# Channel attention over a 113 MB image on one core: the first six rows of the last store go as three transfers of fewer partitions

## The chip, the cores and the metric

The kernel runs on one core of a Trainium2 chip. The metric is the device time of one execution in microseconds (us), the median of several runs. Three runs of the kernel before gave 720.6, 720.0 and 720.54 us, a median of 720.54 us. The profile is of one more execution, which took 720.05 us; its span, from the first recorded instruction to the last, is 718.3 us.

## What is computed

```python
x, w1d   # x: bf16 (1, 384, 384, 384), last axis = channels; w1d: bf16, one number
g = einsum("bhwc->bc", x) / (H * W)        # mean of each channel
s = sigmoid(g * w1d[0])                    # k = 1: no neighbours
out = x * s[:, None, None, :]
```

Every element of the output needs the mean of its channel, so all of x has to be read before the first output element can be made. x has 113 MB and the kernel's on-chip tile holds 275 of its 1152 rows (the unit of the next section), so most of x is read twice.

## The kernel before, in words

The image is seen as 1152 rows of 384 channels for each of 128 partitions (147,456 pixels over 128). All data lives in one on-chip tile, `arena`, of 128 partitions by `ROWS` rows by 384 channels; a row is 768 bytes of one partition.

The rows of x are divided into four runs (`RUNS`, L226): run 0 has the first `N_FIRST` = 43 rows, the next has the rest of what is streamed, and the last two hold what stays on chip. Inside a run of n rows each partition owns n neighbouring rows of DRAM (`view`, L213), so a transfer of m rows of a run moves one piece of m x 768 bytes for each partition it covers.

The work has two halves. In the first, loads bring all rows of x in; TensorE sums them over the partitions (`sum_rows`), and some rows are kept, partly folded so that four rows take the place of three (`fold`). Then ScalarE makes s. In the second half every row is multiplied by s on VectorE (`scale`, L482, its instruction on L487) and stored (`store`, L493, its DMA on L499): first the rows that were kept, unfolded where needed (`unfold`), and then the streamed rows, loaded once more (`load`, L248, its DMA on L255) and stored. Streamed rows are taken from the end of x towards its beginning, so run 0 is the last to be loaded, scaled and stored.

All loads and stores are issued by SyncE (SP), in program order. `Flow` (from L21) records each step with what it reads and writes and puts in the waits; each SP transfer takes one of 24 semaphores in turn (`LANES`), and a transfer also waits for the one 24 before it on the queue. At the end SP waits for the last transfer of each of the 24. A transfer's semaphore counts to 16.

The order of loads, scalings and stores in the second half comes from a planner at build time, the `while True` loop at the end. It keeps its own clock `now`, puts transfers with an estimated cost into `moves`, and a finished scaling into `waiting` by `send(at, a, n, then)`: `at` is the first row of x, `a` the place in the arena, `n` the number of rows. When such an entry is due, the loop calls `store(at, a, n)` (L751). A load is cut into parts of at most `PART` = 16 rows for scaling; run 0 with its 43 rows is scaled as 14, 14 and 15 rows and sent as one store with `at` = 0. It is the only store with `at` = 0, and it is the last transfer of the program.

Of the kernel before, what the change touches and what calls it, by code (L numbers as in the profile page):

```python
# [129 lines left out]
def kernel(  # L130
# [11 lines left out]
    nc = tc.nc  # L142
    P = nc.NUM_PARTITIONS
# [50 lines left out]
    arena = pool.tile([P, ROWS, C], bf16, name="arena")  # L194
# [13 lines left out]
    of = out.rearrange("b h w c -> (b h w) c")  # L208
# [4 lines left out]
    def view(t, r0, n):  # L213
        return t[r0 * P : (r0 + n) * P, :].rearrange("(p r) c -> p r c", r=n)

    def rows(lo, n):
        return [("a", r) for r in range(lo, lo + n)]
# [11 lines left out]
    def run_of(i):  # L229

        return next(run for run in reversed(RUNS) if i >= run[0])
# [171 lines left out]
    def copy_bank(src, dst, reads, writes):  # L403
        fl.add(
            "ACT", lambda: nc.scalar.copy(dst.bitcast(u32), src.bitcast(u32)), reads=reads, writes=writes  # L405
        )

    for i, bk in enumerate(banks):
        lo, hi = i * BANK, min((i + 1) * BANK, PS * C)
# [72 lines left out]
    def scale(a, n, eng="DVE", s=s_bf, after=()):  # L482
        v = arena[:, a : a + n, :]
        vec = nc.vector if eng == "DVE" else nc.gpsimd
        fl.add(
            eng,
            lambda: vec.tensor_tensor(  # L487
                out=v, in0=v, in1=s[:, None, :].to_broadcast([P, n, C]), op=Op.mult
            ),
            reads=rows(a, n) + ["s_bf" if s is s_bf else "bank0"], writes=rows(a, n), after=after,  # L490
        )

    def store(at, a, n):  # L493
        r0, m = run = run_of(at)
        lo, hi = at - r0, at - r0 + n
        assert hi <= m
        return fl.add(
            "SP",
            lambda: nc.sync.dma_start(out=view(of, *run)[:, lo:hi, :], in_=arena[:, a : a + hi - lo, :]),  # L499
            reads=rows(a, hi - lo), dma=True,  # L500
        )

    def unfold(k, first):

        g, lo, p = pieces[k]
        a, at = first + 3 * lo, first + 3 * GROUPS[g][1] + lo
        w, wc = flat(a, 3 * p), [rows(a + j * p, p) for j in range(3)]
        w0, w1, w2 = (flat(a + j * p, p) for j in range(3))
        ba, ca = Y, Y + PIECE
        u, b, c = flat(at, p), flat(ba, p), flat(ca, p)  # L510
        uc, bc, cc = rows(at, p), rows(ba, p), rows(ca, p)

        def fields():
            bits(u, w2, SHR, 3, AND, 0x0F00, wc[2], uc)
            bits(b, w0, SHR, 7, OR, 0x780F, wc[0], bc)
            bits(c, w1, SHR, 11, OR, 0x78F0, wc[1], cc)
            join(b, b, c, AND, bc + cc, bc)
            join(u, u, b, Op.add, uc + bc, uc)

        def three():  # L520
            wall = wc[0] + wc[1] + wc[2]
            bits(w, w, AND, 0x87FF, OR, 0x3800, wall, wall)
            scale(a, 3 * p)

        def fourth():

            bits(u, u, AND, 0x87FF, XOR, 0x3F77, uc, uc)
            scale(at, p + (at + p == first + N_BANKED - 1 and g == BANKED))

        return [  # L530
            (fields, 3 * TS(p) + 2 * TT(p)),
            (three, TS(3 * p) + TT(3 * p)),
            (fourth, TS(p) + TT(p)),
        ]
# [4 lines left out]
    def TT(n):  # L539
        return 0.15 + 0.2 * n  # L540
# [55 lines left out]
    BIG, CAP, PART, LOW, LAST = 32, 48, 16, 9.0, 4.0  # L596
    BANKS_AT = 2
    N_SPLIT = 2
    now = dve_at = 0.0
    moves, waiting, over, acts = deque(), deque(), deque(), deque()  # L600
    landed = deque()
# [7 lines left out]
    def runs():  # L609
        near = {i for g in list(line)[:N_NEAR] if g in TOPS for i in range(TOPS[g], TOPS[g] + GROUPS[g][1])}  # L610
        got, i = [], 0
        while i < ROWS:
            if idle[i] and i not in near:
                j = i
                while j < ROWS and idle[j] and j not in near:
                    j += 1
                got.append((j - i, i))
                i = j
            else:
                i += 1  # L620
        return got

    def send(at, a, n, then, known=None):

        waiting.append((dve_at, n, then, at, a, [] if known is None else known))

    def backlog():
        return sum(e[1] for e in moves) + ROW * sum(e[1] for e in waiting)
# [10 lines left out]
    def stored(a, n):  # L639

        def f():
            for i in range(a, a + n):
                unused.discard(i)
                if not Y <= i < Y + 8:
                    idle[i] = True
        return f
# [30 lines left out]
    def start_group():  # L677
# [35 lines left out]
        sent = 0  # L713
        if len(line) >= total - N_SPLIT and q == PAIR:

# [7 lines left out]
    while True:  # L723

        if dve_at <= now:
            ahead = backlog()
            can = bool(turns)
            if not can and not alongside and (ahead >= PENDING or not landed):
                can = start_group()
            if landed and (ahead < PENDING or not can):  # L730
                a, at, n, end = landed.popleft()
                scale(a, n, s=s_ps if alongside and now else s_bf)
                dve_at = now + TT(n)
                since = (a, at) if since is None else since
                if end or ahead < MERGE:
                    b, first = since
                    send(first, b, at + n - first, stored(b, at + n - first))
                    since = None
            elif can:
                f, t, then = turns.popleft()  # L740
                f()
                dve_at = now + t
                if then:
                    then()
        if alongside and alongside[0][0] <= now:
            _, a, at, n = alongside.popleft()
            store(at, a, n)
            moves.append([now + LAT, n * ROW + PER_STORE, stored(a, n)])
        while waiting and waiting[0][0] <= now:
            _, n, then, at, a, known = waiting.popleft()  # L750
            known.append(store(at, a, n))  # L751
            moves.append([now + LAT, n * ROW + PER_STORE, then])
        if not asked and not line and not turns:
            verdict()
            asked = True
        if out_rows == total and not checked:
            checked = True
            fl.add("POOL", again, reads=["odd_i", "s_bf"], writes=rows(Y, N_OVER), after=written, bare=True)
        while over and over[0][0] <= now:
            over.popleft()[1]()  # L760

        got = runs()
        if bank_at is None and len(line) <= total - BANKS_AT and got and max(got)[0] >= N_BANKED:
            a = max(got)[1]
            for i in range(a, a + N_BANKED):
                idle[i] = False
            back = arena[:, a : a + PS, :].rearrange("p r c -> p (r c)")
            for i, bk in enumerate(banks):
                lo, hi = i * BANK, min((i + 1) * BANK, PS * C)
                copy_bank(bk[:, 0 : hi - lo], back[:, lo:hi], [("bank", i)], rows(a, PS))  # L770
            for lo, hi, at, cell in PARTS:
                copy_bank(at, arena[:, a + N_BANKED - 1, lo:hi], [], rows(a + N_BANKED - 1, 1) + [cell])
            bank_at = (a, now + 5.0)
            got = runs()

        if got and todo < N_STREAM:
            n, a = max(got)
            left = N_STREAM - todo
            left -= run_of(left - 1)[0]
            n = min(n, CAP, left)  # L780
            ahead = backlog()
            if (todo or not (landed or alongside or waiting)) and (n >= BIG or n == left or (ahead < LOW and n >= 8) or ahead < LAST):

                lo = N_STREAM - todo - n
                load(lo, a, n)
                for i in range(a, a + n):
                    idle[i] = False
                parts = [(a + e, lo + e, f - e, f == n) for e, f in split(n, PART)]
                todo += n
                moves.append([now + LAT, n * ROW + PER_LOAD, lambda parts=parts: landed.extend(parts)])  # L790

        if moves and moves[0][0] <= now:
            moves[0][1] -= DT
            if moves[0][1] <= 0:
                over.append((now + SEEN, moves.popleft()[2]))
        else:
            stall += DT
        if not (alongside or moves or waiting or over or landed or line or turns) and todo == N_STREAM:
            break
        now += DT  # L800
# [34 lines left out]
```

## Time and profile before

| | |
|---|---|
| median of three runs | 720.54 us (720.0 to 720.6) |
| the profiled execution | 720.05 us |
| its span | 718.3 us |
| HBM read, written | 189.92 MB, 113.25 MB |
| mean DMA rate over the span | 422 GB/s |
| busy share: PE, DVE, ACT, POOL | 30%, 68%, 17%, 1% |
| the last store's issue, and its size | 691.8 us, 4128 KB |

How to read it: times are counted from the start of the span. Engines are PE (TensorE), DVE (VectorE), ACT (ScalarE), POOL (GpSimd), SP (SyncE). DMA work is done by 16 DMA engines that all queues share; a DMA share of 1.00 (or 100%) over a stretch means that all 16 were moving packets all the time. A packet is counted whole in the stretch in which it starts, so that the share of a short stretch can be somewhat above or below the true one. "DMA to landing" is the time from SP's issue to the last count of the transfer's semaphore; where earlier transfers still wait on the DMA engines, it includes that waiting.

### The profile page before, as it was taken

How to read it: one execution, taken by the hardware profiler on the slowest of the kernel's cores; microseconds unless marked ns; L12 is line 12 of the kernel's file. 1: busy time of each engine (PE TensorE's matmuls, PEld its weight loads, DVE VectorE, ACT ScalarE, POOL GpSimd, SP SyncE). 2: the span in 40 equal slices, each digit the busy share in tenths (PEclk: the TensorE clock that was granted, in tenths of full speed). 3: DMA queues.
4: the chain of work that ended last, by engine and by line, in shares of the span. 5: the costliest groups of instructions: out<-in, count | busy, mean ns of one | idle time of the engine just before them, and what ended most of it. 6: DMA issues, size and time to landing. Idle time of an engine off the chain costs nothing.

```text
span 718.3 us, 2042 instructions
## 1 busy us (share of the span) xinstructions
PE 213.0 (30%) x1186; PEld 0.3 (0%) x3; DVE 485.6 (68%) x454; ACT 122.1 (17%) x101; POOL 10.2 (1%) x7
## 2 busy tenths in 40 slices
PE   4776977997868770000000000000000000000000
PEld 0000000000000000000000000000000000000000
DVE  4606270639896819998997999996991999005640
ACT  3604160426674610000002000000000000000000
POOL 0000000000000005000000000000000000000000
PEclk9989889999999995555555555555555555555555
DMA  9999999999999989999999999999999999999997
GB/s 372 443 422 444 434 431 418 447 428 424 428 426 428 425 343 359 413 424 430 425 434 429 433 443 424 435 426 437 434 431 432 443 431 426 436 429 431 447 421 307
DMA packets 21181, 303.30 MB, mean 422 GB/s; under 512 B 2354, under 2 KB 2738, under 8 KB 9010
## 3 DMA queue, kind: packets, MB, share of 16 engines
q1 hardware_dynamic: 21168, 303.18, 98.9%
q8 instruction: 4, 0.07, 0.0%
q14 instruction: 7, 0.06, 0.0%
q10 hardware_dynamic: 2, 0.00, 0.0%
HBM read 189.92 MB, written 113.25 MB: 422 GB/s over the span
## 4 chain that ended last, share of the span: by engine, by line
DMA 54%; DVE 27%; PE 7%; ACT 3%; another core or an unknown queue 2%; POOL 1%; SPq 1%; issue 1%; DVEq 0%; ACTq 0%
DMA arena<-in_x_dram 38%; DVE arena L487 19%; DMA out_dram<-arena 16%; PE bank L261 7%; DVE arena L295 6%; DVE arena L301 3%; ACT arena L332 2%; POOL arena L487 1%; SPq L255 1%; ACT arena L405 1%; SPq L499 0%; ACT s_bf L475 0%; ACT bank L479 0%; ACT bank L405 0%
## 5 line engine op out<-in xcount | busy, mean ns | idle before, releaser
L487 DVE TENSOR_TENSOR arena<-arena,s_bf 128x1536 bf16<-128x1536 bf16 (+9 forms) x100 | 231.0, 2345 | 84.4 <-DMA arena<-in_x_dram 68.2
L261 PE MATMUL bank<-arena,ones 128*128 128x384 bf16 x1151 | 207.1, 341 | 46.7 <-DMA arena<-in_x_dram 46.2
L295 DVE TENSOR_SCALAR arena<-arena 128x1536 uint16<-128x1536 uint16 (+3 forms) x240 | 142.9, 644 | 111.4 <-DMA arena<-in_x_dram 94.9
L332 ACT ACTIVATE arena<-arena 128x3072 uint16<-128x3072 uint16 (+1 forms) x40 | 108.0, 2700 | 111.0 <-DVE arena L295 111.0
L301 DVE TENSOR_TENSOR arena<-arena 128x1536 uint16<-128x1536 uint16 (+2 forms) x100 | 109.3, 1093 | 7.9 <-PE bank L261 4.0
L557 PE MATMUL bank<-odd,ones 128*128 128x1 bf16 x1 | 0.2, 185 | 313.8 <-DVE odd L552 313.8
L405 ACT COPY arena<-bank 128x512 uint32<-128x512 uint32 (+3 forms) x9 | 4.4, 497 | 107.9 <-DMA out_dram<-arena 107.6
L487 POOL TENSOR_TENSOR arena<-arena,s_bf 128x1536 bf16<-128x1536 bf16 (+1 forms) x3 | 10.0, 3351 | 269.4 <-ACT bank L479 269.4
L487 DVE TENSOR_TENSOR arena<-arena,bank 128x1536 bf16<-128x1536 bf16 (+3 forms) x8 | 9.4, 1250 | 0.0
L405 ACT COPY bank<-arena 128x512 uint32<-128x512 uint32 (+3 forms) x9 | 4.1, 494 | 26.3 <-PE bank L261 26.2
L332 ACT ACTIVATION_READ_ACCUMULATOR arena<-arena 128x1 f32 x40 | 7.5, 186 | 0.0
L261 PE MATMUL bank<-zeros,ones 128*128 128x384 bf16 x32 | 5.5, 326 | 0.0
L475 ACT ACTIVATE s_bf<-bank,w_sc 128x384 bf16<-128x384 f32 x1 | 0.6, 580 | 13.9 <-PE bank L261 13.9
L275 PE MATMUL bank<-arena,ones 128*128 128x384 bf16 x1 | 0.5, 477 | 7.2 <-DMA arena<-in_x_dram 7.2
L803 ACT ACT_TABLE_LOAD x1 | 1.3, 1283 | 0.7 <-PEq L819 0.7
L362 DVE TENSOR_SCALAR w_sc<-bank 128x1 f32<-128x1 f32 x1 | 0.2, 159 | 1.1 <-PE bank L357 1.1
L352 DVE MEMSET ones<- 128x128 bf16 x1 | 0.2, 165 | 1.0 <-SPq L107 1.0
L357 PE MATMUL bank<-w_bf,ones 1*128 1x1 bf16 x1 | 0.2, 178 | 2.2 <-DMA w_bf<-in_w1d_dram 2.2
L557 PEld LDWEIGHTS bank<-odd,ones 128*128 128x128 bf16 x1 | 0.1, 103 | 572.9 <-DVE odd L552 572.9
L561 DVE CAST odd_i<-bank 128x1 int32<-128x1 f32 x1 | 0.2, 157 | 0.3 <-PE bank L557 0.3
L479 ACT COPY bank<-s_bf 128x192 uint32<-128x192 uint32 x1 | 0.3, 323 | 0.0
L547 DVE TENSOR_REDUCE worst<-seen 128x1 f32<-128x40 f32 x1 | 0.2, 188 | 0.0
(8 smaller groups left out, 0.9 us busy)
## 6 DMA issues: line engine op xcount, KB each, us to landing
arena<-in_x_dram SPq DMA_DIRECT2D x16, 4608.0 KB, 29.9
out_dram<-arena SPq DMA_DIRECT2D x9, 3072.0 KB, 24.1
out_dram<-arena SPq DMA_DIRECT2D x5, 4608.0 KB, 35.8
arena<-in_x_dram SPq DMA_DIRECT2D x7, 2304.0 KB, 19.8
arena<-in_x_dram SPq DMA_DIRECT2D x14, 1152.0 KB, 17.0
arena<-in_x_dram SPq DMA_DIRECT2D x5, 3072.0 KB, 15.2
arena<-in_x_dram SPq DMA_DIRECT2D x18, 768.0 KB, 8.9
arena<-in_x_dram SPq DMA_DIRECT2D x2, 4512.0 KB, 29.4
```

The lines of the kernel that those rows point to most:

```text
L255: lambda: nc.sync.dma_start(out=arena[:, a : a + hi - lo, :], in_=view(xf, *run)[:, lo:hi, :]),
L261: return pe.add_instruction(mybir.InstMatmult(name=nc.get_next_instruction_name(), ins=[pe.lower_ap(rhs), pe.lower_ap(ones[:])], outs=[pe. ...
L275: return nc.tensor.matmul(acc, lhsT=ones[:], rhs=arena[:, i, :], start=first, stop=last)
L295: lambda: nc.vector.tensor_scalar(out=dst, in0=src, scalar1=s0, scalar2=s1, op0=op0, op1=op1),
L301: "DVE", lambda: nc.vector.tensor_tensor(out=dst, in0=a, in1=b, op=op), reads=reads, writes=writes
L332: lambda: nc.scalar.activation(out=y, in_=y, func=ACTF.Copy, accum_out=seen[:, 2 * k + i : 2 * k + i + 1]),
L405: "ACT", lambda: nc.scalar.copy(dst.bitcast(u32), src.bitcast(u32)), reads=reads, writes=writes
L475: lambda: nc.scalar.activation(out=s_bf[:], in_=acc, func=ACTF.Sigmoid, scale=w_sc[:, 0:1]),
L479: "ACT", lambda: nc.scalar.copy(s_ps.bitcast(u32), s_bf[:].bitcast(u32)), reads=["s_bf"], writes=["bank0"]
L487: lambda: vec.tensor_tensor(out=v, in0=v, in1=s[:, None, :].to_broadcast([P, n, C]), op=Op.mult),
L557: lambda: nc.tensor.matmul(votes, lhsT=ones[:], rhs=odd[:], start=True, stop=True),
L803: nc.scalar.preload_act_table(ACTF.Sigmoid)
```

## The change

The store with `at` = 0 is written as four stores of the same bytes: three of the first six rows, for the partitions 0 to 12, 13 to 63 and 64 to 127 (13, 51 and 64 partitions), and one of the other 37 rows for all 128 partitions. All other stores are as before.

```diff
-    def store(at, a, n):
+    def store(at, a, n, p0=0, p1=P):
         r0, m = run = run_of(at)
         lo, hi = at - r0, at - r0 + n
         assert hi <= m
         return fl.add(
             "SP",
-            lambda: nc.sync.dma_start(out=view(of, *run)[:, lo:hi, :], in_=arena[:, a : a + hi - lo, :]),
+            lambda: nc.sync.dma_start(
+                out=view(of, *run)[p0:p1, lo:hi, :], in_=arena[p0:p1, a : a + hi - lo, :]
+            ),
             reads=rows(a, hi - lo), dma=True,
         )
+
+    def store_last(at, a, n):
+
+        for p0, p1 in zip(LAST_CUTS, LAST_CUTS[1:]):
+            store(at, a, N_LAST, p0, p1)
+        return store(at + N_LAST, a + N_LAST, n - N_LAST)
...
+    N_LAST, LAST_CUTS = 6, (0, 13, 64, P)
...
-            known.append(store(at, a, n))
+            known.append((store if at else store_last)(at, a, n))
             moves.append([now + LAT, n * ROW + PER_STORE, then])
```

The planner's entry in `moves` stays one entry of 43 rows.

## The prediction, made before the result was known

> **What bounds the kernel now.** I read the page's 40 slices first, then what SP issues at the end, then the packets of the last microseconds. The slices:
>
> ```profile
> span 718.3 us, 2042 instructions
> DMA  9999999999999989999999999999999999999997
> GB/s 372 443 422 444 434 431 418 447 428 424 428 426 428 425 343 359 413 424 430 425 434 429 433 443 424 435 426 437 434 431 432 443 431 426 436 429 431 447 421 307
> ```
>
> The DMA engines are full throughout; only the last slice, 18 us, falls to 307 GB/s. So what the change can win or lose lies in the tail. SP's last stores (start, duration; then issue to landing) and VectorE's last scalings:
>
> ```profile
> 680.15 0.33 SPq L499 DMA_DIRECT2D out_dram<-arena  x1
> 682.85 8.90 DVE L487 TENSOR_TENSOR arena<-arena,s_bf 128x5376 bf16<-128x5376 bf16 x3 [2.73 <-DMA arena<-in_x_dram]
> ...
> 691.78 0.33 SPq L499 DMA_DIRECT2D out_dram<-arena  x1
> ...
> DMA to landing us min/median/max: 24.9/25.9/26.8
> ```
>
> The store ahead of the last is issued at 680.15 and lands 26.8 us later, at 707.0; the last is issued at 691.78 and lands 24.9 us later, at 716.7. For some 15 us the last store only waits behind others, so VectorE and SP are not what ends the kernel: the DMA engines are. Now the tail's packets, in two stretches, 712.7 to 713.36 and 713.36 to 716.36:
>
> ```profile
> DMA packets 14, 0.00 MB, mean 0 GB/s; under 512 B 14, under 2 KB 14, under 8 KB 14
> ...
> DMA packets 6, 0.13 MB, mean 44 GB/s; under 512 B 2, under 2 KB 2, under 8 KB 2
> q1 hardware_dynamic: 6, 0.13, 10.2%
> ```
>
> Every transfer of the SP queue has 128 data packets, one for each partition, and 16 closing packets of a few bytes: the page counts 21168 packets for 87 loads and 60 stores, 144 each.
>
> ```profile
> q1 hardware_dynamic: 21168, 303.18, 98.9%
> q10 hardware_dynamic: 2, 0.00, 0.0%
> ...
> L255 SPq DMA_DIRECT2D arena<-in_x_dram x87: 327/340/1241, 1.0 to 627.3; - x87
> ...
> L499 SPq DMA_DIRECT2D out_dram<-arena x60: 332/332/1252, 270.0 to 691.8; - x60
> ```
>
> So a transfer has one closing packet for each DMA engine it uses, 8 partitions to an engine; w_bf's, of one partition (q10), has one data and one closing packet: one engine. In the tail, then, **fourteen engines close the last store between 712.7 and 713.36, and two close it only about 716.3**, after two data packets each that start after 713.36 (0.13 MB in 4). The kernel ends 3 us later than fourteen of its sixteen DMA engines do. From the last closing at 716.3 it is 0.4 us to the landing, 1.6 more to the end of the span, and 1.75 from there to the 720.05 us of this execution, which stands 0.5 us under the median of 720.54. I add my difference to the median.
>
> **The change part by part.** What an engine takes for one packet comes from stretches with packets of one size (share x 16 x length / packets). Stretches 708 to 712, 695 to 697.5, and 282.9 to 284.3:
>
> ```profile
> q1 hardware_dynamic: 56, 1.85, 106.9%
> ...
> q1 hardware_dynamic: 44, 1.22, 112.8%
> ...
> q1 hardware_dynamic: 146, 0.56, 103.1%
> ```
>
> 33 KB: 1.069 x 64 / 56 = 1.22 us. 27.7 KB: 1.128 x 40 / 44 = 1.025 us. Both are 27 GB/s, so the 37 rows that remain, 28,416 bytes, take 1.05. In the third stretch 130 data packets of 4.3 KB take 0.176 each (16 closings at about 0.01 taken off): 0.18 for the six rows' 4,608 bytes. The two late engines run alone after 713.36 and still need 1.22 (10.2% of 48 engine-us over 4).
>
> *The last store before:* 8 x 1.22 + 0.01 = 9.78 us on each engine.
>
> *After:* each engine has 8 x 1.05 = 8.41 us of the 37 rows, plus small packets. How many depends on how 13, 51 and 64 partitions are divided. The rows show 128 in 16 shares of 8 and 1 as one share, and I take equal shares over as many engines as go into the count: 13 engines of one, 3 of seventeen (51 = 3 x 17), 16 of four. If the engines are always taken from the first on, three have 1 + 17 + 4 = **22 small packets**, ten have 5 and three have 4. [...]
>
> *What a small packet costs* is the open term. Lower end 0.18, from the row above, where each engine serves its own eight partitions. Upper end 0.36, half the rate, if the 27 GB/s belongs not to the engine but to the way into its partitions and two engines must share it. The 64 partitions are what eight engines serve in a full transfer, and sixteen would read them; the 51 belong mostly to engines other than the three, which read them at the same time. No row shows an engine on another's partitions. Two rows are near. A load (639.5 to 644.5) and a store (650.5 to 655.5), both of 36,864-byte packets:
>
> ```profile
> q1 hardware_dynamic: 63, 2.32, 107.4%
> ...
> q1 hardware_dynamic: 64, 2.36, 109.1%
> ```
>
> Both give 1.364 us (1.074 x 80 / 63 and 1.091 x 80 / 64). A limit that is the same for reading HBM and writing it, with sixteen engines at work or two, sits at the engine or at its way into the arena. And small packets at half rate do occur, at 284.4 to 285.9, from a cause that the trace doesn't show: 0.957 x 24 / 79 = 0.29 us for 4 KB.
>
> ```profile
> DMA packets 86, 0.32 MB, mean 213 GB/s; under 512 B 7, under 2 KB 7, under 8 KB 86
> q1 hardware_dynamic: 86, 0.32, 95.7%
> ```
>
> The trace doesn't choose. I take **0.36** as somewhat likelier, since all its full rates are of engines that each have eight partitions to themselves, which the change ends. [...]
>
> *Sum with 0.36.* An engine with 22: 8.41 + 7.92 + 0.04 of closings = 16.37, against 9.78: +6.6. It starts with the fourteen, so it closes not at 712.7 to 713.36 but at 719.3 to 719.95. The late engines with 5: 8.41 + 1.80 + 0.03 = 10.24: +0.46, at 716.8. The last closing moves from 716.34 to 719.3 to 719.95, +3.0 to +3.6; I take +3.4.
>
> *Sum with 0.18.* With 22: 8.41 + 3.96 + 0.04 = 12.41, +2.6, closing at 715.3 to 716.0. Late with 5: 9.34, -0.44; with 4: -0.63. Last closing at 715.9 or so: -0.4.
>
> *The rest.* Three more issues on SP, 0.33 us each, at most 1.25 (the row of L499): 3.8 us at worst, under the 15 us in which the last store waits anyway, so nothing; without that cover up to 3.8. They read rows of the first scaling only (14 rows, 682.85 on, a third of 8.90 us) and can go about 686, ahead of the 37 rows at 691.78; nothing on SP stands between. Their added waits are for transfers 24 back, long landed, and nothing waits for these stores but the end. Closings: one or two more for an engine, 0.01 each, counted above.
>
> **The rivals.**
>
> *A. Small packets keep 0.18 and the late pair is lightened: -0.4.* For it: 27 GB/s is also what an engine alone does, and the three heavy engines fill just the 3 us in which they idle now. Against it: the sharing above. 720.54 - 0.4 = 720.1.
>
> *B. Small packets keep 0.18, but one of the late pair is among the three heavy ones: slower.* No view tells which engines are late. Its place is a late engine with 22 packets; its price is 22 x 0.18 + 8.45 - 9.78 = +2.6 from 716.07 or 716.34: +2.3 to +2.6, 722.8 to 723.1. It decides as soon as a late engine has more than (8 x 0.17) / 0.18 = 7.5 small packets. By count a pair out of 16 misses three given ones in 13 x 12 / (16 x 15) = 65%, so 35%. [...]
>
> *C. B's mishap with 0.36 as well:* 716.34 + 6.6, so +6.6: 727.1.
>
> *D. The division is not in equal shares:* 51 goes as four to an engine on thirteen. Then most engines have 9 small packets, and with 0.18 a late one takes 8.41 + 1.62 + 0.03: +0.3, 720.8 at most.
>
> *E. The lag belongs to the profiled execution alone.* Then the heavy engines would end 2.6 us or more behind the others where none does now. But without the lag the timed runs would be 3 us shorter than 720.05, and they are 720.0 to 720.6.
>
> **How the numbers follow.** I give the shared way 0.55 and the engine's own rate 0.45. By the count of 35%, the first parts into the forecast, 0.36, and C, 0.19. Of the second, 0.05 goes to D and 0.03 to a gain that I don't see (a late engine still has at least 8.41 + 0.72, so -0.63 is the most this balance can give), and the other 0.37 parts into A, 0.25, and B, 0.12. The likeliest is +3.4: **723.9 us**, with its own range 722.6 to 726.0 (a price somewhat under 0.36, or engines slowed in turn on their own partitions). The range reaches down to A with the most it can give, 719.8, and up to 726.0; it leaves out C and the unseen gain. A measurement of this kernel can tell about 0.2%, 1.4 us, from no change: slower by more than that are the forecast, B and C, 0.67; within it A and D, 0.30; faster 0.03.
>
> **What the profile of the changed kernel would show.** The SP queue has 150 transfers, and beyond the full ones' packets 128 small data packets and 13 + 3 + 16 closings if the shares are equal, 13 + 13 + 16 or so in D. In the tail the last closings are three instead of two in the forecast, at about 719.5, with the late pair between them and the others; in A all sixteen close between about 712.4 and 716. The share while small packets run, some 14 us ahead of the end, shows their price directly: 0.18 or 0.36. It would be wrong if the waiting behind earlier stores did not cover the issues (a gap in the DMA share before the last store), or if the late engines were other than two in the timed runs.

## The result and the profile after

The kernel with the change takes 721.78 us, the median of 22 runs (720.87 to 722.99); the kernel before took 720.48 us in 22 runs beside it (719.81 to 722.54). The ratio is 1.0020 with a 95% interval of 1.0015 to 1.0026: 1.3 us slower, and the interval lies above 1; the time is inside the stated range of 719.8 to 726.0, and 38% of the forecast +3.4. The profiled execution took 721.28 us, 1.23 more than that of before.

The page after, its span, slices and SP's queue:

```profile
span 719.5 us, 2045 instructions
...
DMA  9999999999999989999999999999999999999996
GB/s 367 440 425 442 432 432 427 438 430 426 425 428 427 424 340 362 413 424 428 428 432 429 434 433 435 432 431 441 422 443 423 430 437 434 441 430 424 436 428 290
DMA packets 21341, 303.30 MB, mean 422 GB/s; under 512 B 2386, under 2 KB 2770, under 8 KB 9170
...
q1 hardware_dynamic: 21328, 303.18, 98.8%
```

And the count of packets before:

```profile
DMA packets 21181, 303.30 MB, mean 422 GB/s; under 512 B 2354, under 2 KB 2738, under 8 KB 9010
```

The last slice differs most (290 in place of 307 GB/s); no other differs by more than 13. SP's queue has 160 packets more: 128 small ones, and 32 closing packets (2386 against 2354). 32 is 13 + 3 + 16: the transfers of 13, 51 and 64 partitions went over 13, 3 and 16 engines, in the equal shares that the prediction took. With the three always among the thirteen, three engines had 22 small packets; the packets followed by engine, below, agree.

SP's last four issues, and the times from issue to landing of these four stores:

```profile
686.12 1.58 SPq L499 DMA_DIRECT2D out_dram<-arena  x3
...
692.05 0.37 SPq L499 DMA_DIRECT2D out_dram<-arena  x1
...
DMA to landing us min/median/max: 22.5/24.2/25.9
```

The three cut transfers are issued 6 us ahead of the 37 rows, as forecast; their 1.58 us on SP lie wholly inside that gap. Now the tail of the DMA engines, in the stretches 712.5 to 713.2, 713.2 to 716.4, and 716.4 to 717.7:

```profile
DMA packets 13, 0.14 MB, mean 203 GB/s; under 512 B 8, under 2 KB 8, under 8 KB 8
...
DMA packets 19, 0.40 MB, mean 124 GB/s; under 512 B 5, under 2 KB 5, under 8 KB 5
...
DMA packets 4, 0.03 MB, mean 22 GB/s; under 512 B 3, under 2 KB 3, under 8 KB 3
```

Before, fourteen engines closed in one block and two 3 us later. After, eight close in the block, five up to 716.4 and three behind it, the last at 717.6: 1.27 us later than the 716.34 of before, which is the whole difference of the two executions. The packets can be followed engine by engine, since each starts where the last one of its engine ended (within 0.01 us in the last store of the kernel before), and the sizes in each engine's row are known. The closings at 717.6, 716.9 and 715.5 are then those of the three heavy engines (22 small packets); those at 716.5, 715.85 and 714.8 belong to three engines that were already late ahead of the last store and have 5. So two of the three heavy engines close last, and the third closes ahead of two of the late ones.

What a small packet cost, from the stretches 702.5 to 704.5 and 704.5 to 709 of the kernel after:

```profile
DMA packets 127, 0.95 MB, mean 473 GB/s; under 512 B 30, under 2 KB 30, under 8 KB 93
q1 hardware_dynamic: 127, 0.95, 112.0%
...
DMA packets 138, 1.82 MB, mean 405 GB/s; under 512 B 17, under 2 KB 17, under 8 KB 82
q1 hardware_dynamic: 138, 1.82, 100.6%
```

In the first stretch, 63 small packets (93 - 30): 35.8 engine-us, less 0.66 MB of large packets at 27 GB/s (24.4) and closings (0.3), leave 0.18 us each. In the second, 65: 72.4 less 56.3 less 0.2 leave 0.245 each, or 0.23 if the three large packets that took 1.24, 1.24 and 1.57 us there in place of 1.05 are counted as they were. While nearly all engines are at small packets they cost 0.18 us, as in the kernel before; once most engines have gone on to the 37 rows, the ones that still do small packets pay more, 0.23 to 0.245. Followed by engine, the 22 packets of the three heavy engines cost 0.178, 0.234 and 0.246 us in the mean, with single packets up to 0.48. At 0.178 the two heavy engines that close last would have closed at 716.1 and 715.7, and the end would have been the 716.5 of a late engine: their dearer packets are 1.1 of the 1.27 us.

### The profile page after: what moved, and what is told of

Its sections match the earlier page's. It is cut to its first block, busy times and chain, and to the rows that moved or that the text cites. A ratio compares the mean times of both kernels' runs of the same rounds, so it can differ in the third digit from the quotient of the medians.

```text
span 719.5 us, 2045 instructions
## 1 busy us (share of the span) xinstructions
PE 213.1 (30%) x1186; PEld 0.3 (0%) x3; DVE 485.7 (68%) x454; ACT 122.1 (17%) x101; POOL 10.2 (1%) x7
## 2 busy tenths in 40 slices
DMA packets 21341, 303.30 MB, mean 422 GB/s; under 512 B 2386, under 2 KB 2770, under 8 KB 9170
## 4 chain that ended last, share of the span: by engine, by line
DMA 57%; DVE 25%; PE 7%; ACT 3%; another core or an unknown queue 2%; POOL 1%; SPq 1%; issue 1%; DVEq 0%; ACTq 0%
DMA arena<-in_x_dram 41%; DVE arena L487 17%; DMA out_dram<-arena 16%; PE bank L261 7%; DVE arena L295 5%; DVE arena L301 3%; ACT arena L332 2%; POOL arena L487 1%; SPq L255 1%; ACT arena L405 1%; SPq L499 0%; ACT s_bf L475 0%; ACT bank L479 0%; ACT bank L405 0%
## 5 line engine op out<-in xcount | busy, mean ns | idle before, releaser
L475 ACT ACTIVATE s_bf<-bank,w_sc 128x384 bf16<-128x384 f32 x1 | 0.6, 581 | 13.9 <-PE bank L261 13.9
```

Of the source, the lines that this page charges most:

```text
L475: lambda: nc.scalar.activation(out=s_bf[:], in_=acc, func=ACTF.Sigmoid, scale=w_sc[:, 0:1]),
```

## The experiments

Four theories are compared. The **own-rate theory** is rival A: a packet costs what its engine needs, wherever it reads. The **shared-way theory**: an engine that reads partitions which another engine is reading at that time divides with it a way of the 27 GB/s that an engine had in the kernel before (33,024 bytes in 1.22 us). The **heavy-engine theory**: the three engines with 22 packets are last by their count. The **cutting theory**: each added transfer costs something whoever carries it. Ratios are to the kernel before, run beside them (720.31 to 720.34 us); the diffs are against the kernel after, and where one diff has several values, a comment names the run of each.

### Cut in rows alone, and even cuts

```diff
-    N_LAST, LAST_CUTS = 6, (0, 13, 64, P)
+    N_LAST, LAST_CUTS = 6, (0, P)          # e1_rows_only
+    N_LAST, LAST_CUTS = 6, (0, 16, 64, P)  # e2_even_cuts
```

> The last store as two transfers, six rows and 37 rows, both of all 128 partitions: the cut in rows alone. Heavy-engine theory (the three engines that get 22 small packets end the kernel): each engine has 8 small and 8 large packets, so no engine is heavier than before and the time is that of before, 720.5 us, ratio 1.000. Cutting theory (each added transfer costs by itself, whoever carries it; three added cost 1.3 us): one added, +0.4 us, ratio 1.0006.

> Same number of transfers as the change (four), same six rows, but cut at 16 and 64: 16, 48 and 64 partitions, which go in equal shares of 1, 3 and 4 to all sixteen engines. Heavy-engine theory: 8 small packets on every engine at 0.18 us, nothing is heavier, 720.5 us, ratio 1.000. Cutting theory: as the change, +1.3 us, ratio 1.0018. Shared-way theory (small packets take up to 0.36 us as soon as engines read partitions that others also read): all engines pay, up to 8 x 0.18 = +1.4 us.

Cut in rows alone: 720.33 us, ratio 1.0000 (0.9991 to 1.0009). The smaller packets and one more transfer cost nothing that the interval shows. Even cuts: 721.10 us, ratio 1.0012 (1.0003 to 1.0021), +0.8 us, with no engine heavier than another. So the heavy engines are not needed for a loss. This run alone doesn't tell the shared way from the cutting theory, whose +1.3 lies inside the interval; the next two do. It is not all the small packets that pay, either. The tail with even cuts, 713.7 to 719.2:

```profile
DMA packets 11, 0.20 MB, mean 36 GB/s; under 512 B 4, under 2 KB 4, under 8 KB 4
```

Four engines close after 713.7, the last two at 717.0 and 717.3. Followed by engine, thirteen had eight packets at 0.18 (one of them at 0.185); the late pair, which does its small packets while the others are at the 37 rows, had 0.26, which is 8 x 0.08 = 0.65 us more and most of the loss. Some of their last packets of the store ahead, which is not cut, stretched too, from 0.629 us up to 0.76, some 0.2 us on each. One engine that was on time had 0.27 and still closed at 714.0, far from last.

### Twelve rows in place of six, and three

```diff
-    N_LAST, LAST_CUTS = 6, (0, 13, 64, P)
+    N_LAST, LAST_CUTS = 12, (0, 13, 64, P)  # e3_twelve_rows
+    N_LAST, LAST_CUTS = 3, (0, 13, 64, P)   # e6_three_rows
```

> The change with twelve rows in place of six in the three cut transfers. Heavy-engine theory at the engine's own rate: 22 packets of 9,216 bytes at 0.347 and 8 of 31 rows at 0.88, 14.7 us against 9.78, +4.9 on engines that end at 713.3 in the kernel before: last closing at 718.2, +1.9 us or ratio 1.0026. With the sharing that the change showed (0.25 in place of 0.18) scaled to the size, up to 22 x 0.14 = 3 us more: +4.9 us, ratio 1.007. Cutting theory: as the change, +1.3 us.

> The change with three rows in the three cut transfers in place of six, 40 in the rest. Heavy-engine theory: 22 packets of 2,304 bytes at 0.093 and 8 of 30,720 at 1.14 are 11.2 us against 9.8, +1.4, and with half of the change's extra for sharing +2.1, so the heavy engines close at 715.5 and the late pair, hardly lightened, at 716.2 to 716.5: 720.5 us within 0.2, ratio 1.000. Cutting theory: as the change, +1.3 us, since the transfers are as many.

Three rows: 720.14 us, ratio 0.9998 (0.9989 to 1.0007), as many transfers as the change and no loss. Six: +1.3 us. Twelve: 728.87 us, ratio 1.0115 (1.0099 to 1.0130), +8.5 us. The cutting theory, by which the three would be equal, falls. The twelve rows also exceed what I had put as the most with sharing, +4.9: the price does not scale with the size (the dearest mean, below, is 0.36 us over 0.347; with six rows it was 0.07 over 0.178). From the stretch 710 to 719 of the kernel with twelve rows:

```profile
DMA packets 108, 1.73 MB, mean 192 GB/s; under 512 B 19, under 2 KB 19, under 8 KB 19
```

The 192 GB/s are under half of the 442 to 462 of the kernel before in its last store, and single packets of 9,216 bytes, 0.347 us in the kernel before, took up to 1.45. Followed by engine, two heavy engines paid 0.68 and 0.71 us a packet in the mean and closed at 726.0 and 726.5; the third paid 0.347 and closed at 718.4.

### The whole store in 64, 32 and 16 partitions

```diff
     def store_last(at, a, n):
         for p0, p1 in zip(LAST_CUTS, LAST_CUTS[1:]):
-            store(at, a, N_LAST, p0, p1)
-        return store(at + N_LAST, a + N_LAST, n - N_LAST)
+            got = store(at, a, n, p0, p1)
+        return got
...
-    N_LAST, LAST_CUTS = 6, (0, 13, 64, P)
+    N_LAST, LAST_CUTS = 6, (0, 64, P)                     # e5_halves
+    N_LAST, LAST_CUTS = 6, (0, 32, 64, 96, P)             # e8_quarters
+    N_LAST, LAST_CUTS = 6, tuple(range(0, P + 1, 16))     # e12_sixteens
```

> The whole last store, all 43 rows, as two transfers of 64 partitions (0 to 63, 64 to 127). Each goes in 16 equal shares of 4, so every engine still moves 8 packets of 33,024 bytes and none is heavier. Own-rate theory (a packet costs what its engine needs, 1.22 us, wherever it reads): 720.5 us, ratio 1.000. Shared-way theory (27 GB/s belong to the way into eight partitions, and engines that read there together divide it): sixteen engines on the ways of eight, 2.44 us a packet, the last store takes 19.6 in place of 9.8 us, +9.8 us, ratio 1.0136.

> The whole last store, all 43 rows, as four transfers of 32 partitions, each in 16 shares of 2. Own-rate theory: 720.5 us, ratio 1.000. Shared-way theory with a way for each eight neighbouring partitions, as the full transfers divide them: sixteen engines on four ways, 4 x 9.8 us, +29 us, ratio 1.041. [...]

> The whole last store, all 43 rows, as eight transfers of 16 partitions, one to each engine. Halves and quarters both cost 8.4 us. If any transfer of fewer than 128 partitions goes at half rate, these cost 8.4 us too, ratio 1.012. [...] Own-rate theory: nothing.

Here every engine moves 8 packets of 33,024 bytes, as before, and only the partitions are dealt out otherwise. Halves: 728.73 us, ratio 1.0117 (1.0102 to 1.0133), +8.4 us. Quarters: 728.80, 1.0116 (1.0101 to 1.0132), the same. Sixteens: 731.89, 1.0158 (1.0141 to 1.0175), +11.6. The stretch 717.2 to 718.7 with halves:

```profile
DMA packets 14, 0.43 MB, mean 286 GB/s; under 512 B 1, under 2 KB 1, under 8 KB 1
q1 hardware_dynamic: 14, 0.43, 133.8%
```

13 packets of 33 KB took 1.338 x 24 / 13 = 2.47 us each, against 1.22 in the kernel before. **The own-rate theory falls**: with the same bytes and the same count on every engine, a packet took twice as long. Not all pay: followed by engine, two on-time engines and two late ones kept 1.22 throughout, and the other twelve had 2.1 to 2.6 in the mean. A rival, that a transfer of fewer than 128 partitions is slow by itself, doesn't fit one packet in the stretch 707.6 to 707.7 with halves:

```profile
q1 hardware_dynamic: 1, 0.02, 94.2%
```

It is one of a late engine, 16,896 bytes of the store ahead, which has all 128 partitions, and took 0.942 x 1.6 = 1.51 us in place of 0.629. So the price also falls on a packet of an uncut transfer while the halves are being read. No run tells the side of the partitions from that of the DRAM addresses written. That quarters cost as much as halves (+8.5 and +8.4) speaks against a way for each eight neighbouring partitions, by which they would have cost +29; why they cost the same, no run shows. The sixteens, +11.6, don't agree with a fixed half rate (+8.4) either. Shares and rates over 4 us from 704 on, with sixteens (the last rows of the store ahead are still in the first):

```profile
704.00:708.00 4.00, 0.00 (x0) 0.00 (x0) 0.00 (x0) 0.00 (x0) 0.00 (x0) 0.50 1.34 350
708.00:712.00 4.00, 0.00 (x0) 0.00 (x0) 0.00 (x0) 0.00 (x0) 0.00 (x0) 0.50 0.96 206
712.00:716.00 4.00, 0.00 (x0) 0.00 (x0) 0.00 (x0) 0.00 (x0) 0.00 (x0) 0.50 0.79 223
716.00:720.00 4.00, 0.00 (x0) 0.00 (x0) 0.00 (x0) 0.00 (x0) 0.00 (x0) 0.50 1.04 215
```

And two rows of the kernel before:

```profile
704.00:708.00 4.00, 0.00 (x0) 0.00 (x0) 0.00 (x0) 0.00 (x0) 0.00 (x0) 0.50 1.02 442
708.00:712.00 4.00, 0.00 (x0) 0.00 (x0) 0.00 (x0) 0.00 (x0) 0.00 (x0) 0.50 1.07 462
```

The last column is GB/s, and the one before it the share of the DMA engines: from 708 on the rate is 206 to 223, about half of the 442 to 462 of the kernel before, while the engines are at work nearly all the time (0.96, 0.79 and 1.04). Why the sixteens cost 3.2 us more than the halves stays open.

### The cut transfers behind the 37 rows

```diff
     def store_last(at, a, n):
+        store(at + N_LAST, a + N_LAST, n - N_LAST)
         for p0, p1 in zip(LAST_CUTS, LAST_CUTS[1:]):
-            store(at, a, N_LAST, p0, p1)
-        return store(at + N_LAST, a + N_LAST, n - N_LAST)
+            got = store(at, a, N_LAST, p0, p1)
+        return got
...
     N_LAST, LAST_CUTS = 6, (0, 13, 64, P)                 # e7_cut_last
+    N_LAST, LAST_CUTS = 6, (0, 16, 64, P)                 # e9_even_last
+    N_LAST, LAST_CUTS = 12, (0, 13, 64, P)                # e10_twelve_last
```

> The same four transfers as the change, but the 37 rows of all partitions are issued first and the three cut transfers last, so that the heavy engines do their small packets when the others have ended their own. Heavy-engine theory with sharing: bytes and counts are those of the change, but only the late engines are still reading, so the extra of sharing (about 1.5 us on two heavy engines) falls away: 1.3 to 1.7 us under the change, 720.1 to 720.5, ratio to before 0.9995 to 1.000. Cutting theory, or heavy engines by count alone without sharing: as the change, +1.3 us, ratio 1.0018.

> The even cuts (16, 48 and 64 partitions, 8 small packets on each engine) issued behind the 37 rows in place of ahead of them. Shared-way theory: the on-time engines do their small packets together, each for itself, and the late ones when nothing else reads, so the 0.87 us that the even cuts cost ahead of the 37 rows fall away: 720.4 us, ratio 1.000. Cutting theory: as ahead, +0.9 us, ratio 1.0012.

> Twelve rows in the three cut transfers of 13, 51 and 64 partitions, issued behind the other 31 rows; ahead of them they cost +8.5 us. Heavy engines at their own rate, without sharing: 22 x 0.347 + 8 x 0.884 = 14.7 us against 9.8, +4.9 on engines that otherwise close at 713.3, so 718.2 against 716.3: +1.9 us, ratio 1.0026. If the three heavy engines hinder each other too, up to half as much again for the 17 packets, +5 us. Cutting theory: as ahead, +8.5 us.

The change with its order turned round: 720.33 us, ratio 1.0002 (0.9992 to 1.0011). The same packets on the same engines, and the 1.3 us are gone; the interval lies wholly under that of the change. So the heavy-engine theory, as a matter of the count alone, falls as well. From 712.9 to 716.6 of it:

```profile
DMA packets 77, 0.33 MB, mean 90 GB/s; under 512 B 15, under 2 KB 15, under 8 KB 75
q1 hardware_dynamic: 77, 0.33, 23.6%
```

60 small packets (75 - 15), 2 large and 15 closings took 14.0 engine-us; less the large ones, 1.38 and 1.22, and 0.1 for closings, that is 0.19 us a small packet. With most engines done, two heavy engines read at their own rate and closed at 715.2 and 715.6; the third had 0.204 in the mean, with one packet of 0.65. From 716 to 718 there are three small packets and the last closing:

```profile
DMA packets 4, 0.01 MB, mean 7 GB/s; under 512 B 1, under 2 KB 1, under 8 KB 4
```

They are those of the third heavy engine, which closed at 716.55, behind the late pair at 715.98 and 716.0. Twelve rows behind the rest cost +4.4 us (724.69 us, ratio 1.0056, 1.0042 to 1.0069), half of the 8.5 ahead of it but more than the +1.9 of their own rate: the heavy engines still pay behind the rest, 0.347, 0.417 and 0.460 a packet in the mean.

**The even cuts behind the rest miss my expectation**: 721.24 us, ratio 1.0012 (1.0003 to 1.0021), as much as ahead of it. Where the loss went can be seen in the stretch 714.1 to 714.4:

```profile
DMA packets 2, 0.06 MB, mean 189 GB/s; under 512 B 0, under 2 KB 0, under 8 KB 0
q1 hardware_dynamic: 2, 0.06, 74.7%
```

These are the last large packets of the late pair: 0.747 x 4.8 / 2 = 1.79 us each in place of 1.05. So the late pair loses 0.74 us there, and its own small packets behind them cost 0.18. The on-time engines, done with their own rows, are at their small packets from 711.6 to 714.06; but by the trace the two stretched packets start at 714.12 and 714.36, when those engines have just closed. Why these two packets are long stays open. Against the shared-way theory as I had put it, the miss stands.

### Which engines are late

```diff
-    N_LAST, LAST_CUTS = 6, (0, 13, 64, P)
+    N_LAST, LAST_CUTS = 1, (0, 15, 29, 42, 54, 65, 75, 84, 92, 99, 105, 110, 114, 117, 119, 120, P)
```

The first kernel (e4_marks) has the marks ahead of the other 42 rows, the second (e11_marks_last) behind them, with the order turned round as above.

> One row (768 bytes) of the last store goes in sixteen transfers of 15, 14, 13 and so on down to 1 partitions, and one of 8; the other 42 rows as one. With equal shares on the engines from the first on, the first has 16 packets of 768 bytes and the last none, each engine another number, so that the late ones can be told in the trace. Heavy-engine theory: at most 8 packets of 0.036 more than eight, +0.3 us on engines that are not late; the time stays within 0.3 us of before. Cutting theory: fifteen transfers more than before's one and 37 rows' worth, 16/3 of 1.3 us, +7 us.

> The sixteen transfers of one row that mark the engines by their number of packets, issued behind the other 42 rows. Ahead of them they cost +1.6 us, and the two late engines had 13 and 12 packets, which makes them the fourth and fifth from the first. If the late pair belongs to a place and not to chance, the last two closings are again of engines with 13 and 12 packets. Time: sixteen issues of about 0.64 us on SP, 10 us, fit into the 15 us of waiting; small packets of 0.036 and their closings on the late ones 0.6 us: 720.4 to 721.0.

The marks ahead: 721.96 us, ratio 1.0025 (1.0015 to 1.0034); behind: 722.86, ratio 1.0033 (1.0021 to 1.0045). Both miss: I had expected at most 0.3 and 0.7 us. With one row the small packets stay at 0.036, and in the first kernel it is large packets that stretch, from 1.19 us up to 2.19; in the second the end is only 0.7 us later than in the kernel before (717.0 in place of 716.3) and the rest of its 2.5 us comes after the last packet, from a span of 720.9 and 2.0 us outside it. Why stays open. The marks did tell the late engines. The stretch 716.4 to 717.1 of the second kernel, in which only the late pair is left:

```profile
DMA packets 52, 0.02 MB, mean 28 GB/s; under 512 B 27, under 2 KB 52, under 8 KB 52
```

25 small packets (52 - 27) for the two. Followed by engine, one has 13 and one 12, as in the first kernel: the fourth and the fifth engine from the first. In the trace of the change, too, the engines that were late ahead of the last store had 5 small packets, as the fourth to the thirteenth have.

## Why the prediction was right and wrong

**Right:** where the end is (the DMA engines' tail, the whole difference there); the 15 us that cover SP's issues; the equal shares and so 22, 5 and 4 packets; that heavy engines close last, though two of them and not three; the sign; and that packets of the cut transfers can cost more than the engine's own rate (0.234 and 0.246 us in the mean on two heavy engines, against 0.178). Rival A, the engine's own rate and a gain of 0.4, falls with the halves. Rival B, a late engine among the heavy ones, falls with the marks, and C with it: the three heavy engines are the first three, the late pair comes right behind them. D falls with the 32 closings. E, the lag in the profiled execution alone, no run tests; the profiles of the kernel before, of the change and of both kernels with marks have late engines (closing at 716.07 and 716.34 in the first, against 713.34 and earlier for the others).

**Wrong: the size of one term**, "what a small packet costs". I took 0.36 us for all 22 packets of a heavy engine. That was an estimate, twice the measured 0.18, and no run shows it as their mean. The halves had the doubled price (2.47 us against 1.22); in the change, measured means on the three heavy engines are 0.178, 0.234 and 0.246: 22 x 0.246 + 8.46 = 13.9 us from 703.75, closing at 717.6, where the prediction had 16.4 and 719.3 to 719.95. Two things keep the price down. While all engines are at their small packets together, they cost 0.18 (702.5 to 704.5). And of the later ones not all pay: the third heavy engine had 0.178 throughout. Why just that one went free stays open.

**Also off, and hidden by that:** the prediction let a late engine with 5 packets close at 716.8 by 5 x 0.36; it closed at 716.5, with 5 at 0.22 to 0.23. Its five packets cost 0.28 us more than at 0.178, and it came to the last store at 706.9, 0.3 us later than the latest engine of before (706.6). So of the relief that the change could give the late engines, 0.44 us at their own rate, nothing was left. With the cut transfers last the late pair did get some: it closed at 715.98 and 716.0, in place of 716.07 and 716.34, although its last packets of the 37 rows took 1.22 and 1.38 in place of 1.05. There the third heavy engine closed last, 0.2 us behind the end of before, by one packet of 0.65. Why the relief was so small, no run shows.

No kernel of the study beats the one before; the three that equal it are the cut in rows alone, the change with three rows and the change with its order turned round.

## What to carry to other kernels

Before moving work between DMA engines by cutting a transfer into partition ranges, count two things: how many engines each piece gets (equal shares: 51 partitions went to three), and whether several engines will then read one range of partitions (in the two halves most packets took 2.1 to 2.6 us in the mean of their engine, in place of 1.22). The same bytes on the same engines cost 1.3 us ahead of a full transfer and nothing behind it, and a store of all rows in two halves of 64 partitions took nearly twice its time (+8.4 us on 9.8). An idle stretch of 3 us at the tail was not 3 us to be had here: in both orders tried, the packets given to the idle engines came with packets dearer than at the rate of the kernel before: ahead, 0.234 and 0.246 us in the mean on two of those engines in place of 0.178; behind, 1.22 and 1.38 on the late pair in place of 1.05.

## What the runs showed of the hardware that I had not expected

- The last store of the kernel before kept 442 to 462 GB/s (704 to 712); cut in ranges of 64, 32 or 16 partitions it falls to 206 to 289 while the most engines are at work, although all 16 have equal work (halves: 278, 239 and 289 in the three stretches of 4 us from 704 on; quarters: 258 and 277 in two of 5 us from 705 on; sixteens: 206 to 223 in three of 4 us from 708 on).
- The extra cost falls on engines and packets unevenly: with halves four engines kept 1.22 us a packet while twelve had 2.1 to 2.6; of small packets in the change some took 0.18 and others up to 0.48 beside each other, and with twelve rows single 9,216-byte packets took up to 1.45 in place of 0.347.
- The late pair was the fourth and fifth engine in both kernels with marks (13 and 12 small packets). What makes them late stays open.
